# Retention and two feed-forward layers on one core: a negation moved, weights' stores one hop later, eight weight blocks kept on the chip

## The chip, the cores and the metric

The kernel runs on one core of one Trainium2 chip. The metric is the device time of one execution in microseconds (us). Five engines work side by side, each with its own instruction queue: TensorE (PE, matrix products), VectorE (DVE), ScalarE (ACT), GpSimd (POOL) and SyncE (SP), which in this kernel issues every transfer between the chip's memory (SBUF) and device memory (DRAM). Products accumulate in PSUM banks.

## The reference, cut to what matters

```
q, k, v: 4 batches, 8 heads, 576 positions, 64 per head
D[i, j]  = gamma_h ** (i - j) for i >= j, else 0
attn     = (q @ k.T / 8 * D) @ v                    # no softmax
x        = attn as 2304 tokens x 512
h        = x @ w_in                                 # 512 -> 2048
g        = max(h, 0) + alpha * min(h, 0)            # one alpha per unit
x2       = g @ w_out                                # 2048 -> 512
gate     = sigmoid(x2 @ w_gate); val = x2 @ w_val   # 512 -> 1536 each
out      = (gate * val) @ w_out2                    # 1536 -> 512
```

## The kernel before

**Numbers.** Each fp32 operand of a feed-forward product is split into a high and a low part, and a product is three matmuls (high by high, high by low, low by high; `products`, L632). `split` (L202, L203) makes the parts: ACT copies the source rounded (high), DVE subtracts that from the source (low).

**Tokens** are cut into blocks of 256, 512, 512, 512, 512. Block 0 and 1 run first, with the attention's chunks (up to 128 positions) in front of and between them; then block 2, in which the attention of 3 and 4 and the second layer's weights are prepared; then blocks 3 and 4 together in eight double steps (`h_step`), which use sums of weights and fewer products; then the y products of these, the second layer for the pairs of blocks, and block 0's second layer at the end.

**The attention.** `att_q` makes a decayed copy of q: ACT writes the factors `dec` (L497, two buffers), POOL multiplies q with it in place (L500). PE makes the scores s (L518), DVE masks them (L522), PE makes o and the state's update m (L537 to L557), DVE adds the update to m_sb (L551, L553), and `split` makes x from o.

**The first layer.** Its weights come as 16 column blocks of the first matrix (m = 0, 512 by 128, index f) and 16 row blocks of the second (m = 1). A block r is loaded as 64-bit words into one of five raw slots (`load_weight`, L217). `to_single` makes fp32 of it: two ACT passes (L225, L226), then on DVE a shift into a buffer (L229), an add (L231) and a sign insertion (L234). For m = 0 the buffer of the shift is also the result, `one`; for m = 1 the result is in the raw slot and the buffer, `top`, is free after the add. `one` and `top` share two buffers of the tag "top". `prepare_weight` then splits the result (ACT L248, DVE L250) into w and stores: `one` (256 KB) to w1f (L254), from which the double steps later make their sums, and the split block (512 KB) to w1d (L257), from which it is read again later. It is a generator; each `yield` ends a hop, and `advance` takes every open generator one hop further between pieces of PE's work. When one has ended, `load_weights` loads the next raw blocks into whatever raw slots are free.

`ffn1_h` makes one h tile (12 products of 4 column parts into a PSUM bank; two banks, ps_h), ACT the two halves of the leaky function (L651, L652), DVE joins them with the unit's −alpha from na_sb (L653), and `split` makes g. `ffn1_y` multiplies g with the row block into four accumulating banks.

**What stays.** 38 slots of 4 KB per partition (`slot`, `free`) serve everything in turn, freed ones going to the end of the line. `uses` counts how many blocks still read a weight: row and column blocks with f < 9 (RES) stay for three blocks, later ones are reloaded from w1d by `fetch`. The double steps take seven slots out (`quarter_slots`, NQ, twice); `load_inner(t)` reads into them, for q = 0 and 1, the split column block 2t+q and half of block 2t+q+8 from w1d, beside the sums that `prepare_sums` makes.

**Order.** PE's order is the program's. The other engines' orders are set by a scheduler when the program is built; `behind(...)` ties an instruction behind an urgent one of its engine (a split of x or g). SP issues its transfers in order: one that waits holds up those behind it.

**The negation.** The alphas are loaded last of the first inputs (L1139), and ACT makes na_sb = −alpha (L1140) right behind in the program.

Of the kernel before, what the change touches and what calls it, by code (L numbers as in the profile page):

```python
# [10 lines left out]
F32 = mybir.dt.float32  # L11
# [19 lines left out]
NSLOT = 38  # L31
NLATE, NWIDE = 2, 8
NRAW = 5
NQ = 7
AHEAD = 2


# [76 lines left out]
def retention_two_ffn(ctx: ExitStack, tc: tile.TileContext, att, cst, alpha, w1, w2, out0, out1):  # L114
# [57 lines left out]
    def free(t):  # L172
        h = held[t.tensor.name]
        h[1] -= 1
        if not h[1]:
            where, _, line = held.pop(t.tensor.name)
            line.append(where)
# [58 lines left out]
    def prepare_weight(key):  # L236
        layer, f, m = key
        raw = raw_w.pop(key)
        if m == 0:
            one = small.tile([P, DM], F32, tag="top", name=f"one{f}_{m}")  # L240
            yield from to_single(raw, one.bitcast(U32))
            free(raw)
        else:
            one = raw[:, :, 0].bitcast(F32)
            yield from to_single(raw)
        yield
        w = slot([P, 2, DM], F32R, f"w{layer}_{f}_{m}")
        nc.scalar.activation(w[:, 0, :], one, AF.Copy)  # L248
        yield
        nc.vector.tensor_tensor(out=w[:, 1, :], in0=one, in1=w[:, 0, :].bitcast(F32), op=ALU.subtract)  # L250
        wt[f, m] = w
        uses[f, m] = PLAIN if f < RES else 2 if f < BESIDE else 1
        if m == 0:
            nc.sync.dma_start(out=w1f[f % NSUM][:, f // NSUM], in_=one)  # L254
        else:
            free(raw)
        nc.sync.dma_start(out=w1d[f, m], in_=w.bitcast(F32))  # L257

    def used(f, m):

# [152 lines left out]
    def load_weights():  # L413
        while to_load and raw_slots:
            load_weight(to_load.pop(0))

    def advance():

        for g in list(under_way):
            with behind("act", "dve"):  # L420
                done = next(g, StopIteration) is StopIteration
            if done:
                under_way.remove(g)
                load_weights()

    def begin_weight():
        if to_prepare and to_prepare[0] in raw_w:
# [361 lines left out]
    def load_inner(t):  # L789

        for q in range(2):
            w = inner[t, q, 1] = slot([P, 2, DM], F32R, f"wi{t}_{q}", quarter_slots)
            nc.sync.dma_start(out=w.bitcast(F32), in_=w1d[2 * t + q, 0])
        w = inner[t, 0, 2] = inner[t, 1, 2] = slot([P, 2, 2, DM // 2], F32R, f"wi{t}_3", quarter_slots)
        for q in range(2):
            nc.sync.dma_start(out=w[:, q].bitcast(F32), in_=w1d[2 * t + q + NSUM, 0][:, :, DM // 2:])
# [3 lines left out]
    def h_step(t, between):  # L800
        bank = bank_of(f"h_{t}", t == 0)
        seen = {}

        def product(ps, m, q, first=False):
            i, place = INNER_AT[m]
            if i == 0:
                need(1, 2 * t + q)
            w = inner[t, q, i]
            if i == 0:
                w = tuple(x[:, place] for x in w)  # L810
            elif i == 1:
                w = tuple(w[:, x, place * 256:(place + 1) * 256] for x in range(2))
            else:
                w = tuple(w[:, q, x] for x in range(2))
            products(
                ps, [
                    (tuple(x[:, k * P:(k + 1) * P] for x in w), tuple(x[:, k] for x in factors[m]))
                    for k in range(2)
                ], first, True, True,
            )  # L820
            for key, n in ((q if i < 2 else 0, i), (4, 2, 2)[i]), (m, 2):
                seen[key] = seen.get(key, 0) + 1
                if seen[key] == n:
                    if key == m:
                        if t == NIN - 1:
                            for x in factors.pop(m):
                                free(x)
                        continue
                    w = inner.pop((t, *key))
                    for x in w if i == 0 else (w,):  # L830
                        free(x)

        for c in range(2):
            for r in range(2):
                gated[t, c, r] = slot([P, 2, DM], F32, f"g{t}_{c}{r}")
        a, b, c, e, es, d = {}, {}, {}, {}, {}, {}

        def out(ps, r, k):
            for q in range(2):
                leaky(gated[t, k, r][:, q], ps[q], 2 * t + q + k * NSUM, f"lt{t}_{r}{k}{q}")  # L840

        for m, q in ((1, 0), (5, 0), (5, 1), (1, 1)) if t == 0 else ((1, 0), (1, 1), (5, 0), (5, 1)):
            x = a if m == 1 else e
            x[q] = bank("ae"[m == 5], q)
            product(x[q], m, q, True)
            between(0)
        for q in range(2):
            b[q] = bank("b", q)
            nc.scalar.activation(b[q], a[q], AF.Copy)
            es[q] = small.tile([P, DM], F32, tag="es", name=f"hes{t}_{q}")  # L850
            nc.scalar.activation(es[q], e[q], AF.Copy)
        between(1)
        for q in range(2):
            product(a[q], 6, q)
            c[q] = bank("c", q)
            nc.vector.tensor_tensor(out=c[q], in0=a[q], in1=es[q], op=ALU.add)
        for q in range(2):
            product(b[q], 2, q)
        between(2)
        out(b, 0, 0)  # L860
        for q in range(2):
            product(a[q], 7, q)
        for q in range(2):
            d[q] = gated[t, 1, 1][:, q]
            nc.vector.tensor_tensor(out=d[q], in0=a[q], in1=es[q], op=ALU.add)
        for q in range(2):
            product(c[q], 3, q)
        between(3)
        out(c, 0, 1)
        for q in range(2):  # L870
            product(a[q], 4, q)
        between(4)

        out(a, 1, 0)
        with behind("act", "dve", ahead=0):
            out(d, 1, 1)
# [260 lines left out]
    for n in runs_of(0) + runs_of(1):  # L1137
        load_chunk(n)
    nc.sync.dma_start(out=al_sb, in_=alpha)  # L1139
    nc.scalar.activation(na_sb, al_sb, AF.Copy, scale=-1.0)  # L1140
    load_weights()

    pa, py = (ps_a, "ab"), (ps_y, "yy")
# [1 line left out]
    done = [0]  # L1145

    def first_h(i):
        while done[0] < EARLY and done[0] * (n0 + n1 - LATE) < EARLY * (i + 1 - LATE):
            ffn1_h(0, done[0])
            done[0] += 1  # L1150
# [43 lines left out]
    for j in range(1, PLAIN):  # L1194
        stages = stages_of(2) if j == 1 else stages_of(3, 4)
        first = step1 if j == 1 else 0
        total = 2 * sum(len(runs_of(i)) for i in ((2,) if j == 1 else (3, 4)))
        span = SPAN * (NF1 - first) // NF1 if j == 1 else SPAN_X
        staged = 0
        for f in range(first, NF1):  # L1200
            fetch(f, 0)
            fetch(f + 1, 0)
            fetch(f, 1)
            ffn1_h(j, f)
            if j < PLAIN - 1 or f < UNTIL:
                second_pace(PACE_S)
            if j == PLAIN - 1 and staged == total:
                if not under_left:

                    for _ in stages:  # L1210
                        pass
                    for x in "ab":
                        ps = ps_a.tile([P, DM], F32, tag=x, name=f"whole{x}")
                        nc.tensor.matmul(ps, wt[f, 1][:, 0, :P], x_t[j][:, 0, 0], start=True, stop=True)
                    att_only.close()
                    pool = ctx.enter_context(tc.tile_pool(name="late", bufs=1, reuse_waits="tile"))
                    spare.extend((pool, f"late{i}") for i in range(NLATE))
                    under_left.append(left_factors(-1))
                else:
                    next(under_left[0], None)  # L1220
            if j == PLAIN - 1 and f == UNTIL:
                quarter_slots.extend(spare.popleft() for _ in range(NQ))
                load_inner(0)
            if j == PLAIN - 1 and UNTIL <= f < UNTIL + 2:
                begin_job((1, f - UNTIL))
            for point in range(2):
                second_step()
                if staged < total and staged * span < total * (2 * (f - first) + point):
                    next(stages)
                    staged += 1  # L1230
                if point == 0:
                    later(BEHIND - 1)
                elif under_left:
                    next(under_left[0], None)
            late.append((j, f))
        for _ in stages:
            pass
# [2 lines left out]
    x_only.close()  # L1240
    pool = ctx.enter_context(tc.tile_pool(name="wide", bufs=1, side="right", reuse_waits="tile"))
    spare.extend((pool, f"wide{i}") for i in range(NWIDE))
    quarter_slots.extend(spare.pop() for _ in range(NQ))

    def in_h(t):
        def between(point):
# [159 lines left out]
```

## Time and profile before

| | before |
|---|---|
| three runs, median (lowest to highest) | 891.17 us (890.69 to 892.07) |
| the profiled execution | 890.89 us |
| its span, first to last instruction | 889.1 us |
| PE busy | 856.2 us, 96% |
| PE's weight loads, beside its products | 716.7 us, 81% |
| DVE, ACT, POOL busy | 566.2, 446.6, 126.5 us |
| moved by DMA | 245.05 MB |
| mean granted clock of PE | 0.995 |

Spans and waits of all views come from the profiled execution. An engine is busy in a row from its start for the length given; rows of one engine may overlap by a tenth of a us where the next starts while the last one drains. In brackets stands the idle time ahead of a row and what ended it. A wait for several things is put down to the one that came last.

### The profile page before, as it was taken

Reading aid. Unit: us, or ns where it says so; the run is one execution under the profiler, and the core shown is the slowest. Engines: PE = TensorE matmul, PEld = TensorE weight load, DVE = VectorE, ACT = ScalarE, POOL = GpSimd, SP = SyncE. Lnnn points to the kernel's source line nnn. Section 1 sums busy time; section 2 is a strip of 40 time slices with the busy share of each in tenths; the row PEclk is TensorE's granted clock in tenths of the full one; section 3 lists DMA queues with packets and bytes.
Section 4 is the critical chain, followed back from the end, with each engine's and each line's share of the span. In section 5 each row is a group of like instructions: output and inputs, shape, how many; then the busy total and the mean of one; then the engine's idle time right before and its main releaser. Section 6 shows DMA issues by size and latency. Waiting matters only on the chain.

```text
span 889.1 us, 13072 instructions
## 1 busy us (share of the span) xinstructions
PE 856.2 (96%) x4770; PEld 716.7 (81%) x4770; DVE 566.2 (64%) x829; ACT 446.6 (50%) x785; POOL 126.5 (14%) x119
## 2 busy tenths in 40 slices
PE   5689989999999999999999999999999999999998
PEld 4578878777887888887888878888888888888897
DVE  2798995577767578888945676368932333496121
ACT  4487874455644566787625555335432222353111
POOL 5100002334621001123531032000000000000000
PEclk9899999999999999999999999999999999999999
DMA  9779999779996545769995999916698563359970
GB/s 306 253 244 368 373 378 348 279 270 302 341 343 245 207 165 189 264 227 362 356 414 188 336 418 405 365 72 213 223 397 286 185 206 123 137 201 356 388 267 24
DMA packets 89679, 245.05 MB, mean 276 GB/s; under 512 B 13072, under 2 KB 16144, under 8 KB 89616
## 3 DMA queue, kind: packets, MB, share of 16 engines
q1 hardware_dynamic: 89616, 244.22, 75.6%
q8 instruction: 38, 0.62, 0.3%
q14 instruction: 25, 0.20, 0.1%
HBM read 176.03 MB, written 68.16 MB: 275 GB/s over the span
## 4 chain that ended last, share of the span: by engine, by line
PE 50%; DMA 5%; DVE 2%; ACT 2%; issue 1%; SPq 0%; ACTq 0%; DVEq 0%
PE a L637 13%; PE yy L637 10%; PE oa L637 7%; PE z L637 4%; PE e L637 3%; DMA r<-w 3%; PE b L637 3%; PE c L637 3%; PE o L637 2%; PE oc L637 2%; PE ob L637 2%; PE oe L637 2%; DMA tq<-td 1%; DMA wo<-wod 1%; DVE q L312 0%
## 5 line engine op out<-in xcount | busy, mean ns | idle before, releaser
L637 PE MATMUL h<-x,w 128*128 128x512 f32 (+1 forms) x432 | 85.5, 348 | 7.6 <-DVE g L203 5.8
L637 PEld LDWEIGHTS h<-x,w 128*128 128x128 f32 x432 | 67.6, 189 | 19.5 <-DVE g L203 7.3
L301 POOL TENSOR_TENSOR r<-r,r 128x256 f32<-128x256 f32 x36 | 46.1, 1288 | 242.7 <-DVE r L234 196.7
L312 DVE TENSOR_TENSOR q<-r,q 128x512 fp32r<-128x512 f32 x72 | 54.6, 784 | 16.2 <-ACT q L311 15.9
L311 ACT ACTIVATE q<-r 128x512 fp32r<-128x512 f32 x72 | 46.2, 671 | 28.7 <-POOL r L301 17.9
L637 PE MATMUL y<-g,w 128*128 128x512 f32 x240 | 58.9, 394 | 0.0
L653 DVE SCALAR_TENSOR_TENSOR h<-h,na_sb,t 128x512 f32<-128x512 f32 (+1 forms) x48 | 32.0, 667 | 37.0 <-ACT h L652 37.0
L225 ACT ACTIVATE r<-r 128x512 f32<-128x512 f32 x68 | 45.6, 670 | 15.7 <-DMA r<-w 15.6
L637 PEld LDWEIGHTS y<-g,w 128*128 128x128 f32 x240 | 44.4, 188 | 10.2 <-issue 1.0
L651 ACT ACTIVATE t<-h 128x512 f32<-128x512 f32 (+1 forms) x48 | 25.0, 521 | 53.9 <-PE h L637 53.8
L963 DVE TENSOR_TENSOR c<-a,es 128x512 f32<-128x512 f32 x24 | 16.7, 697 | 52.4 <-PE a L637 48.7
L226 ACT ACTIVATE r<-r 128x512 int32<-128x512 uint32 x68 | 45.5, 669 | 0.0
L500 POOL TENSOR_TENSOR qk<-qk,dec 128x512 f32<-128x512 f32 (+1 forms) x16 | 20.4, 1278 | 144.2 <-DMA qk<-att 139.0
L231 DVE CUSTOM_DVE_ANT_0 r<-r,top 128x1024 uint16<-128x1024 uint16 x52 | 37.4, 732 | 1.6
L234 DVE SCALAR_TENSOR_TENSOR r<-r 128x512 uint32<-128x512 uint32 x52 | 37.4, 724 | 0.5
L637 PEld LDWEIGHTS z<-x,zp 128*128 128x128 f32 x288 | 36.0, 192 | 0.9
L637 PE MATMUL z<-x,zp 128*128 128x256 f32 x288 | 36.3, 283 | 0.0
L637 PE MATMUL h<-x,v 128*128 128x512 f32 x144 | 35.4, 395 | 0.0
L637 PE MATMUL y<-g,v 128*128 128x512 f32 x144 | 35.2, 393 | 0.0
L202 ACT ACTIVATE g<-h 128x512 fp32r<-128x512 f32 (+1 forms) x48 | 25.1, 522 | 20.1 <-DVE h L653 19.9
L518 PE MATMUL s<-qk 64*128 64x128 f32 (+1 forms) x320 | 23.3, 285 | 12.3 <-POOL qk L500 7.3
L203 DVE TENSOR_TENSOR g<-h,g 128x512 fp32r<-128x512 f32 (+1 forms) x48 | 28.8, 599 | 9.5 <-ACT g L202 9.2
(460 smaller groups left out, 2246.6 us busy)
## 6 DMA issues: line engine op xcount, KB each, us to landing
tq<-td SPq DMA_DIRECT2D x84, 512.0 KB, 8.3
r<-w SPq DMA_DIRECT2D x68, 512.0 KB, 6.6
wo<-wod SPq DMA_DIRECT2D x42, 512.0 KB, 3.5
v<-w1d SPq DMA_DIRECT2D x40, 512.0 KB, 6.1
td<-q SPq DMA_DIRECT2D x36, 512.0 KB, 4.0
w1d<-w SPq DMA_DIRECT2D x32, 512.0 KB, 6.3
wod<-q SPq DMA_DIRECT2D x24, 512.0 KB, 9.6
zp<-td SPq DMA_DIRECT2D x48, 256.0 KB, 5.2
```

The source lines that it names most:

```text
L202: a = nc.scalar.activation(hi, src, AF.Copy)
L203: d = nc.vector.tensor_tensor(out=lo, in0=src, in1=hi.bitcast(F32), op=ALU.subtract)
L225: nc.scalar.activation(high.bitcast(F32), high.bitcast(F32), AF.Copy, scale=2.0 ** -112)
L226: nc.scalar.activation(low.bitcast(I32), low, AF.Copy, scale=2.0 ** -29)
L231: nc.vector.tensor_tensor(out=out.bitcast(I32), in0=low.bitcast(I32), in1=top.bitcast(I32), op=ALU.add)
L234: nc.vector.scalar_tensor_tensor(out, high, 0x80000000, out, ALU.bitwise_and, ALU.bitwise_or)
L301: sub = lambda o, a, b: nc.gpsimd.tensor_tensor(out=o, in0=a, in1=b, op=ALU.subtract)
L311: nc.scalar.activation(part[0], src, AF.Copy)
L312: nc.vector.tensor_tensor(out=part[1], in0=src, in1=part[0].bitcast(F32), op=ALU.subtract)
L637: nc.tensor.matmul(ps, l, r, start=first and i == 0, stop=last and i == len(todo) - 1, skip_group_check=joins)
L651: nc.scalar.activation(t, ps, AF.Relu)
L653: nc.vector.scalar_tensor_tensor(ps, ps, na_sb[:, f:f + 1], t, ALU.mult, ALU.add)
```

## The change

Three things are changed.

a) na_sb's negation is written into `first_h`, which runs between the attention's chunks, ahead of the first h tile, and tied behind ACT's last urgent split. On ACT it then stands behind the split of chunk 5's x and ahead of the first t.

b) In `prepare_weight`, `load_weights` is called where the raw slot becomes free (for m = 0 after the sign insertion, for m = 1 after the subtraction), no longer at the generator's end, and the two stores come one hop later.

c) The first eight column blocks (f < NSUM = 8) are not stored to w1d and are kept in their slots for one more use, in the double steps; `load_inner` no longer reloads them, and the slots taken out for the double steps are five (NQ1) in place of seven.

```diff
-NQ = 7
+NQ, NQ1 = 7, 5
@@ prepare_weight
             yield from to_single(raw, one.bitcast(U32))
             free(raw)
+            load_weights()
...
         wt[f, m] = w
-        uses[f, m] = PLAIN if f < RES else 2 if f < BESIDE else 1
+        stays = m == 0 and f < NSUM
+        uses[f, m] = PLAIN + stays if f < RES else 2 if f < BESIDE else 1
+        if m:
+            free(raw)
+            load_weights()
+        yield
         if m == 0:
             nc.sync.dma_start(out=w1f[f % NSUM][:, f // NSUM], in_=one)
-        else:
-            free(raw)
-        nc.sync.dma_start(out=w1d[f, m], in_=w.bitcast(F32))
+        if not stays:
+            nc.sync.dma_start(out=w1d[f, m], in_=w.bitcast(F32))
@@ advance
                 under_way.remove(g)
-                load_weights()
@@ load_inner
-            w = inner[t, q, 1] = slot([P, 2, DM], F32R, f"wi{t}_{q}", quarter_slots)
-            nc.sync.dma_start(out=w.bitcast(F32), in_=w1d[2 * t + q, 0])
+            inner[t, q, 1] = wt[2 * t + q, 0]
@@ h_step
+                    if i == 1:
+                        used(2 * t + q, 0)
+                        continue
@@ main program
-    nc.scalar.activation(na_sb, al_sb, AF.Copy, scale=-1.0)
     load_weights()
@@ first_h
+        if i == LATE:
+            with behind("act", ahead=0):
+                nc.scalar.activation(na_sb, al_sb, AF.Copy, scale=-1.0)
@@ two places, ahead of the double steps
-                quarter_slots.extend(spare.popleft() for _ in range(NQ))
+                quarter_slots.extend(spare.popleft() for _ in range(NQ1))
...
-    quarter_slots.extend(spare.pop() for _ in range(NQ))
+    quarter_slots.extend(spare.pop() for _ in range(NQ1))
```

PE's order is the same before and after. The order of the other engines moves. In the listings below, lines are those of each version (L250 and L653 of before are L251 and L659 of the change), the two numbers behind a weight's name are its f or m as far as the name keeps them (r_6_0 is column block 6, r_5_1 row block 5), and the last number is the buffer's; one_0_894 of before and one_0_888 of the change are the `one` of block 6.

ACT, at the end of the attention's first chunks, before:

```order
L497 ACTIVATE dec_1784<-c_sb 128x128 x4
L1140 ACTIVATE na_sb<-al_sb 128x16
L497 ACTIVATE dec_1899<-c_sb 128x128 x4
L202 ACTIVATE x_243<-o_327 128x4x128
L225 ACTIVATE r_0_0_230<-r_0_0_230 128x512
```

and with the change, there and at the first h tile:

```order
L503 ACTIVATE dec_1776<-c_sb 128x128 x4
L503 ACTIVATE dec_1891<-c_sb 128x128 x4
L202 ACTIVATE x_242<-o_326 128x4x128
L225 ACTIVATE r_0_0_229<-r_0_0_229 128x512
...
L202 ACTIVATE x_305<-o_517 128x4x128
L1158 ACTIVATE na_sb<-al_sb 128x16
L657 ACTIVATE t_0_553<-h_0_540 128x256
```

The first two dec rows shown are those of chunks 7 and 8, x of o_327 or o_326 is chunk 1's, x of o_517 chunk 5's. The negation left the place between dec of chunk 7 and dec of chunk 8 and stands ahead of the first tile's t.

DVE from the sign insertion of block 6's `one` to that of block 7's, before (the names in brackets are what a row waits for; DMAHW is a transfer):

```order
L234 SCALAR_TENSOR_TENSOR one_0_894<-r_6_0_758,one_0_894 128x512 [waits DVE_49]
L229 TENSOR_SCALAR top<-r_5_1_798 128x512 [waits DMAHW5_49,DMAHW1_49]
L203 TENSOR_TENSOR g_3_852<-h_3_835,g_3_852 128x512 [waits Activation_49]
L231 ISA r_5_1_798<-r_5_1_798,top 128x512x2 [waits DVE_49]
L250 TENSOR_TENSOR w_6_0_924<-one_0_894,w_6_0_924 128x512 [waits Activation_49]
L234 SCALAR_TENSOR_TENSOR r_5_1_798<-r_5_1_798 128x512 [waits DVE_49]
L229 TENSOR_SCALAR one_0_951<-r_7_0_830 128x512 [waits DMAHW4_49]
L653 SCALAR_TENSOR_TENSOR h_4_897<-h_4_897,na_sb,t_4_910 128x256 [waits Activation_49]
```

and with the change:

```order
L234 SCALAR_TENSOR_TENSOR one_0_888<-r_6_0_753,one_0_888 128x512 [waits DVE_49]
L659 SCALAR_TENSOR_TENSOR h_3_831<-h_3_831,na_sb,t_3_844 128x512 [waits Activation_49]
L251 TENSOR_TENSOR w_4_1_886<-r_4_1_695,w_4_1_886 128x512 [waits Activation_49]
L229 TENSOR_SCALAR top<-r_5_1_758 128x512 [waits DMAHW4_49,DMAHW1_49]
L251 TENSOR_TENSOR w_6_0_920<-one_0_888,w_6_0_920 128x512 [waits Activation_49]
L203 TENSOR_TENSOR g_3_848<-h_3_831,g_3_848 128x512 [waits Activation_49]
L231 ISA r_5_1_758<-r_5_1_758,top 128x512x2 [waits DVE_49]
L659 SCALAR_TENSOR_TENSOR h_4_891<-h_4_891,na_sb,t_4_904 128x256 [waits Activation_49]
L229 TENSOR_SCALAR one_0_944<-r_7_0_824 128x512 [waits DMAHW6_49,DMAHW3_49,DVE_49]
```

Block 7's shift into `one_0_944` now waits for two transfers, its own load and the store of block 6's `one`; before, it waited for one.

SP in the same stretch, before:

```order
L217 DMA r_8_0_919<-w 128x1024
L254 DMA w1f_130<-one_0_894 128x512
L217 DMA r_7_1_943<-w 128x1024
L257 DMA w1d_0_104<-w_6_0_924 128x1024
L257 DMA w1d_1_103<-w_5_1_949 128x1024
```

and with the change:

```order
L217 DMA r_7_1_917<-w 128x1024
L262 DMA w1f_130<-one_0_888 128x512
L217 DMA r_8_0_912<-w 128x1024
L264 DMA w1d_1_101<-w_4_1_886 128x1024
L217 DMA r_8_1_972<-w 128x1024
```

The store of block 6's `one` stands behind the load that takes the slot of its raw block, and the column block's split store is gone.

## Rows read from the trace of the kernel before

**Rows 1.** one core, busy us (instructions) by engine, PEclk, DMA share, GB/s, by windows

```profile
40.00:60.00 20.00, 16.20 (x131) 13.79 (x130) 17.98 (x37) 14.77 (x31) 0.00 (x0) 1.00 0.79 282
80.00:100.00 20.00, 19.27 (x115) 17.14 (x116) 18.45 (x36) 15.45 (x31) 0.00 (x0) 1.00 1.01 383
140.00:160.00 20.00, 20.00 (x124) 17.77 (x124) 6.13 (x11) 8.94 (x23) 4.60 (x4) 1.00 0.94 341
...
160.00:280.00 120.00, 116.75 (x940) 93.71 (x942) 86.51 (x139) 62.59 (x128) 47.96 (x46) 1.00 0.85 302
```

**Rows 2.** PE's waits: engine, line, releaser, total us, times, longest

```profile
PE h L637 <- DVE g L203: 5.8, 5, 1.8
```

**Rows 3.** PE's timeline: start, us, what, idle before it

```profile
27.43 0.86 PE L518 MATMUL s<-qk 64*64 64x64 f32 x13 [3.79 <-DVE x L203]
...
59.26 3.01 PE L637 MATMUL h<-x,w 128*128 128x512 f32 x12 [1.83 <-DVE g L203]
...
92.21 3.02 PE L637 MATMUL h<-x,w 128*128 128x512 f32 x12 [0.44 <-DVE g L203]
...
125.90 3.03 PE L637 MATMUL h<-x,w 128*128 128x512 f32 x12 [1.61 <-DVE g L203]
...
401.42 0.50 PE L637 MATMUL a_h<-xx_4h,s7h 128*128 128x512 f32 x1 [0.52 <-DVE g L865]
```

**Rows 4.** DVE's timeline, 60 to 90 us: two waits

```profile
68.54 0.43 DVE L229 TENSOR_SCALAR top<-r 128x512 uint32<-128x512 uint32 x1 [0.93 <-issue]
...
82.49 0.43 DVE L229 TENSOR_SCALAR top<-r 128x512 uint32<-128x512 uint32 x1 [1.25 <-DMA w1f<-one]
```

**Rows 5.** ACT's timeline, 17 to 50 us

```profile
18.98 1.28 ACT L497 ACTIVATE dec<-c_sb 128x128 f32<-128x128 f32 x4 [1.23 <-POOL qk L500]
24.79 0.21 ACT L1140 ACTIVATE na_sb<-al_sb 128x16 f32<-128x16 f32 x1 [4.53 <-DMA al_sb<-alpha]
24.91 1.26 ACT L497 ACTIVATE dec<-c_sb 128x128 f32<-128x128 f32 x4
```

**Rows 6.** POOL's timeline, 17 to 32 us

```profile
18.21 0.73 POOL L500 TENSOR_TENSOR qk<-qk,dec 128x256 f32<-128x256 f32 x1 [0.24 <-DMA qk<-att]
...
23.50 0.72 POOL L500 TENSOR_TENSOR qk<-qk,dec 128x256 f32<-128x256 f32 x1
```

**Rows 7.** DVE's timeline, 72 to 81 us: how long its rows take

```profile
73.29 0.75 DVE L653 SCALAR_TENSOR_TENSOR h<-h,na_sb,t 128x512 f32<-128x512 f32 x1
73.95 0.68 DVE L250 TENSOR_TENSOR w<-r,w 128x512 fp32r<-128x512 f32 x1
74.55 0.69 DVE L234 SCALAR_TENSOR_TENSOR one<-r,one 128x512 uint32<-128x512 uint32 x1
...
77.89 0.42 DVE L229 TENSOR_SCALAR one<-r 128x512 uint32<-128x512 uint32 x1
78.23 0.49 DVE L653 SCALAR_TENSOR_TENSOR h<-h,na_sb,t 128x256 f32<-128x256 f32 x1
78.62 0.68 DVE L231 CUSTOM_DVE_ANT_0 one<-r,one 128x1024 uint16<-128x1024 uint16 x1
...
79.82 0.42 DVE L203 TENSOR_TENSOR g<-h,g 128x256 fp32r<-128x256 f32 x1
```

**Rows 8.** transfers, us to landing: w1f stores issued at 30.38, 53.30, 63.04, 75.55

```profile
w1f<-one SPq DMA_DIRECT2D x1, 256.0 KB, 2.4
...
w1f<-one SPq DMA_DIRECT2D x1, 256.0 KB, 4.1
...
w1f<-one SPq DMA_DIRECT2D x1, 256.0 KB, 5.4
...
w1f<-one SPq DMA_DIRECT2D x1, 256.0 KB, 6.9
```

**Rows 9.** the chain of waits ahead of 401 us

```profile
370.73 4.60 DMA r<-w
```

**Rows 10.** SP's timeline at 267 us

```profile
267.72 0.51 SPq L368 DMA_DIRECT2D b<-w1f  x1
```

## Prediction

> **What bounds the kernel now.** I read the 20 us windows of the first 160 us, then PE's waits, then the timelines of the engines that end them, last the chain of waits. TensorE (PE) is busy 20.00 of 20 us in 140 to 160 and idle for 3.25 us (120.00 − 116.75) in all of 160 to 280 [rows 1], after that only at 401, which is treated below. The change leaves PE's order as it is, so it can only move idle time, and most of that lies ahead of 140. There, between 60 and 140, DVE is the busiest of the others: 18.45 us in 80 to 100, with the DMA engines at a share of 1.01 [rows 1]. PE waits there for DVE's split of g, 5.8 us in five waits [rows 2]: 1.83 us at 59.26, 0.44 at 92.21, 1.61 at 125.90 [rows 3], the other two lie between. PE works an h tile ahead of its y products, and ps_h has two banks, so h tile k needs the g of tile k−2 out of its bank. Whatever delays DVE ahead of those g's lands on PE; DVE's own waits there are 0.93 us at 68.54 and 1.25 us at 82.49 [rows 4], both the shift that opens a weight's preparation and needs a buffer of "top". What an earlier step buys before 125.90 is kept only as far as the next g permits.
>
> **Part a, the negation.** ACT stands 4.53 us before na_sb, waiting for alpha's transfer; dec of chunk 8 and the split of chunk 1's x are queued behind it [rows 5], and PE's next scores wait 3.79 us for that split's DVE half [rows 3]. It looks like 4.5 us to be had. It isn't: dec has two buffers, and dec of chunk 8 takes that of chunk 6, which POOL reads from 23.50 for 0.72, to 24.22 [rows 6]. The pair before shows the step: dec of chunk 7 started at 18.98, right after POOL had ended with the buffer [rows 5]. So dec starts at about 24.26 in place of 24.91, and x's split comes **0.65 us** earlier, not 4.5. In its new place, ahead of the first t, the negation costs ACT 0.12 us (24.79 to 24.91); alpha has long landed by then, so it adds no wait.
>
> **Part b in the attention.** In the rows of 20 to 60 two things differ besides: x of chunk 6 has 1.20 us less of DVE rows ahead of it, and the first matrix's loads are issued a hop sooner. Followed by hand with the old durations, the first h tile of block 1 starts 1.95 us earlier and the split of g(1,1), for which 59.26 waits, 0.65 to 1.2 us earlier; I take **−0.9 us** for PE at 59.26.
>
> **Part b, the stores one hop later.** No store is taken away by this, but the shift's buffer is. A column block's single-precision copy `one` lies in "top"; its store w1f reads it, and the next user but one of the buffer must wait until that store has landed. DVE's rows, from start to start [rows 7]: 0.66 for L653 at 512 columns and 0.39 at 256, 0.60 for the other rows of 512 (73.95 to 74.55), 0.34 for a shift and, being as long (0.42), for g's split at 256. Before, one6's store had 6.00 us of such rows to land in, and still cost 1.25; one4's had 4.60 and cost 0.93. Afterwards the shift of one7 waits for one6's store, with seven rows between (0.66 + 0.60 + 0.34 + 0.60 + 0.60 + 0.60 + 0.39 = **3.79 us**), and that of r_7_1 for one7's, with eight (0.60 + 0.60 + 0.39 + 0.60 + 0.60 + 0.34 + 0.34 + 0.60 = **4.07 us**); one4's keeps 4.60, all others have 5.5 or more. Each store also stands behind one load on SP that the same DVE row releases, about 0.55 us.
>
> So all hangs on how long a 256 KB store takes to land, L. It took 2.4 us when issued at 30.38, 4.1 at 53.30, 5.4 at 63.04, 6.9 at 75.55 [rows 8]. The bytes decide: per pair of weights the kernel of before moves 512 × 4 + 256 KB, and without the column block's split store 512 × 3 + 256, 22% less, until block 8; a DMA share of 1.01 in 80 to 100 would become some 0.8. With a like share, 0.79 in 40 to 60 [rows 1], stands the store of 53.30. I take L = **4.1 us**, and 2.4 and 6.9 as bounds.
>
> The Trainium skill, page "DMA: Bandwidth & Descriptors", section "Anatomy of one DMA — SWDGE (gpsimd) path", gives about 2.0 us fixed plus bytes over 436 GB/s, which for 256 KB is an estimate of 2.6 us. The store of 30.38 agrees with 2.4, that of 75.55, with 6.9, doesn't; by the page's figure none of the new waits would arise, and the time would be that of rival B.
>
> With L = 4.1: one7's shift waits 0.55 + 4.1 − 3.79 = 0.86, r_7_1's 0.55 + 4.1 − 4.07 = 0.58, together 1.44; the old 0.93 + 1.25 = 2.18 go. DVE's order has more weights' rows ahead of some g's: +2.14 us ahead of g(0,6) (for which 92.21 waits), +0.94 ahead of g(0,11) (for which 125.90 waits). At 92.21: −0.9 − 2.18 + 1.44 + 2.14 = +0.5 us, PE later. At 125.90: −0.9 − 2.18 + 1.44 + 0.94 = **−0.7 us** if DVE then has its h in time; PE's +0.5 of 92.21 has waits of 0.73 and 1.61 left in which to disappear, yet DVE takes h from PE, so some of it stays: 0 to −0.7, I take **−0.35**. Each us more of L costs two waits in series at 125.90, and from 4.05 on one4's as a third.
>
> **Part c, eight blocks kept.** Eight stores and eight loads of 512 KB go, 8.4 of 245 MB. In the double steps PE is fed but for one wait of 0.52 at 401.42, for DVE's g [rows 3]; the chain of waits leads to it over a load of r (370.73, 4.60 us) [rows 9] and a store of td. None of these is removed; eight loads fewer lie beside them. Bounds: 0, and 0.7 (the 0.52 and a little around it); I take **−0.3**, since DVE's order there is unchanged and its own rows come between those transfers. The price: slots. Eight are held to the double steps, two of them in place of quarter slots. The load of b on SP at 267.72 [rows 10] comes some 2 us later, because it stands behind a v load that now waits for a slot; its users on DVE come later too, and PE's next need of them is ten us on. I cost this at nothing, and 0.5 to 1 if the cover is gone. The 3.25 us of 160 to 280 I leave as they are: DVE's rows stand in the old order there but for a few.
>
> **Sum.** The profiled execution took 890.89 (span 889.1 and 1.8 around it), 0.28 under the median of 891.17. 890.89 − 0.35 − 0.3 = **890.2 us**.
>
> **Rivals.** *B, the stores land fast.* With L = 3.6 the two waits are 0.36 and 0.08: −0.9 − 2.18 + 0.44 + 0.94 = −1.7 at 125.90, and −0.3 to −0.7 at 401: 888.5 to 888.9. For it: 22% fewer bytes, 2.4 us on an empty queue. Against: r's load of 512 KB goes out just ahead of each store.
>
> *C, the other side: the stores stay slow.* The place is DVE's shifts of one7 and r_7_1, the price 2 to 3 us per us of L; at L of about 4.4 the gain of 125.90 is gone, and from about 5.2 the slowing can be measured. With the 5.4 of 63.04 [rows 8] the waits are 2.16, 1.88 and, at one4's, 1.35, 5.39 in place of 2.18, so −0.9 + 3.21 + 0.94 = +3.2: 890.89 + 3.2 − 0.3 = 893.8. For it: stores of 5.4 to 6.9 in just that stretch of before.
>
> *D, the slots.* b's loads and the td stores behind them come late enough for PE to wait: +0.5 to 1 on the forecast, 890.7 to 891.2.
>
> *E, the negation was the bottleneck after all.* If dec of chunk 8 needn't wait for POOL, x's split comes up to 4.5 us sooner, PE's 3.79 goes, and what the weights' loads let through of it, 1 to 3 us, is kept: 887 to 889. Against it stands the two-buffer rule and the row of 18.98.
>
> **Chances.** Forecast 0.38, D 0.12, B 0.22, E 0.06, C 0.22. What a measurement of this kernel can tell from no change is about 0.2%, 1.78 us: faster is under 889.4, slower over 892.95. B and E, and 0.05 of the forecast, lie below: faster 0.33. Of C 0.19 lies above, the rest is between: slower 0.19, same 0.48. The range leaves out C's upper half and E: **888.2 to 893.6**.
>
> **What would show it.** Right: dec of chunk 8 starting at about 24.3; na_sb without a wait; PE at h(1,2) at 58.3 to 58.7; DVE's shifts of one7 and r_7_1 waiting for a w1f store, by 0.5 to 1 us each, and w1f's landing at 4 us; PE's gap at 401 within 0.5 us of what it was. Wrong: stores of 5 us and more between 60 and 100 (C), none of these waits (B), PE gaps between 160 and 300 that end with a DMA (D).

## The result and the profile after

The changed kernel is slower: 899.12 us (median of 6 runs, 897.60 to 900.95) against 891.66 for the kernel before (6 runs), a ratio of 1.0083 with a 95% interval of 1.0066 to 1.0100. Forecast were 890.2 and a range of 888.2 to 893.6. The profiled execution took 900.35 with a span of 898.6; before these were 890.89 and 889.1.

PE's order is the same in both kernels, so the start of one and the same product can be subtracted between the traces. The first fence is PE's timeline of the changed kernel at the places of [rows 3] (start, us, what, idle time ahead and what ended it) and at four more.

```profile
26.16 0.68 PE L524 MATMUL s<-qk 64*64 64x64 f32 x14 [3.31 <-DVE x L203]
...
57.94 3.06 PE L643 MATMUL h<-x,w 128*128 128x512 f32 x12 [1.83 <-DVE g L203]
80.21 4.28 PE L643 MATMUL h<-x,w 128*128 128x512 f32 x12 [2.08 <-DVE g L203]
94.83 3.01 PE L643 MATMUL h<-x,w 128*128 128x512 f32 x12 [1.51 <-DVE g L203]
104.94 3.06 PE L643 MATMUL h<-x,w 128*128 128x512 f32 x12 [1.51 <-DVE g L203]
...
129.60 3.03 PE L643 MATMUL h<-x,w 128*128 128x512 f32 x12 [0.93 <-DVE g L203]
...
203.49 0.51 PE L643 MATMUL h<-x,w 128*128 128x512 f32 x1 [1.22 <-ACT x L202]
...
286.01 1.64 PE L543 MATMUL o<-qk,m_sb 128*128 128x128 f32 x8 [2.05 <-DVE qk L528]
...
411.10 0.50 PE L643 MATMUL a_h<-xx_4h,s7h 128*128 128x512 f32 x1 [0.57 <-DVE g L873]
```

| the product that started before at | starts after at | difference |
|---|---|---|
| 59.26 | 57.94 | −1.32 |
| 80.30 | 80.21 | −0.09 |
| 92.21 | 94.83 | +2.62 |
| 125.90 | 129.60 | +3.70 |
| 198.22 | 203.49 | +5.27 |
| 278.02 | 286.01 | +7.99 |
| 401.42 | 411.10 | +9.68 |
| the end (span) | | +9.5 |

So PE is 1.3 us early at 58, 5.0 are lost between 58 and 130, and another 6.0 between 130 and 411. The profiled execution is 1.2 us above the median of its kernel and that of before 0.8 under its own, so 2.0 of the 9.5 belong to these two executions. The 1.3 isn't a gain of the change: the product that starts at 8.9 us in the trace of before starts 1.11 earlier here, and 0.6 to 1.4 earlier in each of the other twelve traces, whatever was changed in them.

The first loss is seen in the windows (busy us of PE, PEld, DVE, ACT, POOL, then granted clock, DMA share, GB/s). To set against [rows 1]:

```profile
80.00:100.00 20.00, 18.28 (x95) 15.75 (x96) 16.83 (x34) 15.78 (x32) 0.00 (x0) 0.91 0.79 266
100.00:120.00 20.00, 17.78 (x111) 15.81 (x110) 17.79 (x33) 14.99 (x32) 0.00 (x0) 1.00 0.99 369
```

The DMA share of 80 to 100 fell from 1.01 to 0.79, as reckoned; yet PE did 95 products there in place of 115, and DVE lost time too: 16.83 busy in place of 18.45. DVE's timeline tells on what it stood (the answer to [rows 4]), and the three stores behind that, in the order of their issue at 62.09, 74.02 and 81.49 (the answer to [rows 8]; last column us to landing):

```profile
68.84 0.43 DVE L229 TENSOR_SCALAR top<-r 128x512 uint32<-128x512 uint32 x1 [2.55 <-ACT w L249]
...
78.19 0.43 DVE L229 TENSOR_SCALAR one<-r 128x512 uint32<-128x512 uint32 x1 [0.81 <-DVE h L659]
...
86.88 0.43 DVE L229 TENSOR_SCALAR top<-r 128x512 uint32<-128x512 uint32 x1 [1.72 <-DMA w1f<-one]
```

```profile
w1f<-one SPq DMA_DIRECT2D x1, 256.0 KB, 6.7
...
w1f<-one SPq DMA_DIRECT2D x1, 256.0 KB, 4.1
...
w1f<-one SPq DMA_DIRECT2D x1, 256.0 KB, 5.3
```

The first two waits are put down to another engine, but each ends within 0.1 us of a store's landing: 62.09 + 6.7 = 68.8 and 74.02 + 4.1 = 78.1. These are the three shifts of the prediction, of r_4_1, one7 and r_7_1: 5.08 us in all, where 2.18 had been.

After the wait of 2.08 at 80.21 the granted clock fell to half, to 1.2 GHz (column behind POOL's):

```profile
82.00:83.00 1.00, 1.00 (x3) 0.72 (x3) 1.00 (x3) 0.64 (x2) 0.00 (x0) 0.50 0.87 164
...
288.00:290.00 2.00, 2.00 (x30) 1.97 (x26) 1.20 (x3) 0.10 (x1) 0.00 (x0) 0.53 0.00 0
```

The twelve products at 80.21 took 4.28 us in place of 3.01, and with their successors PE lost 1.6 us there beside its waits. The second row is the stretch behind the wait of 2.05 at 286.01, where another 1.6 went the same way (from +7.99 at 278.02 to +9.58 at the product that started before at 290).

What ACT shows of the moved negation (the answer to [rows 5]):

```profile
23.62 1.28 ACT L503 ACTIVATE dec<-c_sb 128x128 f32<-128x128 f32 x4 [4.03 <-POOL qk L506]
24.80 0.57 ACT L202 ACTIVATE x<-o 128x512 fp32r<-128x512 f32 x1
...
40.49 0.20 ACT L1158 ACTIVATE na_sb<-al_sb 128x16 f32<-128x16 f32 x1
```

ACT stands nearly as long as before (4.03 in place of 4.53), and now for POOL; the negation runs at 40.49 without a wait.

### The profile page after: what moved, and what is told of

It is laid out like the page before. It is cut to its first block, busy times and chain, and to the rows that moved or that the text cites. A ratio compares the mean times of both kernels' runs of the same rounds, so it can differ in the third digit from the quotient of the medians.

```text
span 898.6 us, 13045 instructions
## 1 busy us (share of the span) xinstructions
PE 859.9 (96%) x4770; PEld 719.7 (80%) x4770; DVE 569.1 (63%) x829; ACT 446.9 (50%) x785; POOL 127.3 (14%) x119
## 4 chain that ended last, share of the span: by engine, by line
PE 53%; DMA 3%; DVE 2%; ACT 1%; issue 1%; SPq 0%; ACTq 0%; DVEq 0%
PE a L643 14%; PE yy L643 10%; PE oa L643 7%; PE z L643 4%; PE b L643 4%; PE e L643 4%; PE c L643 3%; PE o L643 2%; PE oc L643 2%; PE ob L643 2%; PE oe L643 2%; DMA r<-w 2%; DMA wo<-wod 1%; DMA td<-q 0%; DVE g L772 0%
## 5 line engine op out<-in xcount | busy, mean ns | idle before, releaser
L659 DVE SCALAR_TENSOR_TENSOR h<-h,na_sb,t 128x512 f32<-128x512 f32 (+1 forms) x48 | 32.0, 667 | 35.4 <-ACT h L658 35.3
L643 PEld LDWEIGHTS y<-g,w 128*128 128x128 f32 x240 | 44.8, 189 | 10.5 <-issue 1.0
L234 DVE SCALAR_TENSOR_TENSOR r<-r 128x512 uint32<-128x512 uint32 x52 | 40.3, 779 | 0.4
L308 POOL TENSOR_TENSOR r<-r 128x256 f32<-128x256 f32 x36 | 34.6, 966 | 3.0 <-DVE r L234 1.4
```

Source lines behind the costliest of these rows:

```text
L234: nc.vector.scalar_tensor_tensor(out, high, 0x80000000, out, ALU.bitwise_and, ALU.bitwise_or)
L308: sub = lambda o, a, b: nc.gpsimd.tensor_tensor(out=o, in0=a, in1=b, op=ALU.subtract)
L643: nc.tensor.matmul(ps, l, r, start=first and i == 0, stop=last and i == len(todo) - 1, skip_group_check=joins)
L659: nc.vector.scalar_tensor_tensor(ps, ps, na_sb[:, f:f + 1], t, ALU.mult, ALU.add)
```

## The experiments

Theory 1 was rival C's: stores one hop later that land late hold the shift's buffer. Theory 2 was rival D's: the slots of the kept blocks. Each part of the change was first put alone into the kernel before, and the waits were taken out of the changed kernel. Ratios are to the kernel before, run beside each (medians of 891.7 to 893.4), with their 95% intervals. "Lost at 125.9" is how much later the product of 125.90 starts than in the profile of before; each is taken from one execution.

**e1, the negation alone.** The diff is that of part a.

> The kernel before with the negation alone moved. Theory 1 (the loss comes from the stores one hop later: a store of 'one' that lands late holds the shift buffer): dec of chunk 8 starts 0.5 to 0.7 us earlier, and 891.7 moves by less than 1 us either way. Theory 2 (the loss comes from the slots that the eight kept blocks hold): the same. Rival E of the prediction (the negation was the bottleneck): 1 to 3 us faster.

890.67 us, ratio 0.9984 (0.9968 to 0.9999), so the part is harmless. By the time alone rival E isn't out, since 890.67 is 1.6 under the 892.23 of before beside it. The trace speaks against it: dec of chunk 8 takes over the wait (ACT's timeline, 17 to 45 us), and PE's wait for x behind it is 3.09 us in place of 3.79.

```profile
23.15 1.28 ACT L497 ACTIVATE dec<-c_sb 128x128 f32<-128x128 f32 x4 [4.33 <-POOL qk L500]
```

**e2, the stores one hop later alone.** The diff is that of part b, with the stores of all 32 split blocks.

> The kernel before with the loads a hop sooner and the stores a hop later alone; all 32 split stores stay. Theory 1: slower by 3 to 6 us, DVE's shifts waiting 4 us and more in all between 60 and 125 us for a w1f store, as the changed kernel does. Theory 2: within 1 us of before, and no more shift waits than the 2.2 us of before.

891.48 us, ratio 0.9983 (0.9967 to 0.9999); the product of 125.90 is 1.8 us early. DVE's waits (engine, line, releaser, total, times, longest; 40 to 140 us):

```profile
DVE h L655 <- ACT h L654: 4.6, 9, 1.1
DVE top L229 <- DMA w1f<-one: 2.2, 2, 1.6
```

The shifts wait 2.2 us for stores, as they did before (0.93 and 1.25), and not the 5 of the changed kernel. DVE now waits most for h, which means that it is no longer the late one. Theory 1 as it stood falls: the later stores by themselves neither bring those waits nor lose anything. What 5 us of them would cost, this run can't tell.

**e3, the kept blocks alone.** The diff is that of part c; loads and stores stay at their old hops.

> The kernel before with the eight blocks kept, alone; loads and stores at their old hops. Theory 1: no new waits ahead of 140 us, since each w1f store goes out as before with fewer bytes beside it; 890 to 892.5, what it loses is between 240 and 290 us, up to 2 us. Theory 2: most of the changed kernel's loss, 5 to 8 us slower, with PE's waits between 150 and 300 us.

899.86 us, ratio 1.0086 (1.0057 to 1.0115): the whole loss. But it isn't where theory 2 has it. PE's waits between 46 and 140 us:

```profile
PE h L639 <- DVE g L203: 10.5, 8, 2.0
```

10.5 us in place of 5.8, and the product of 125.90 is 4.5 us late. At that time no kept block holds a slot longer than before, since every one of them still has its three plain uses ahead. Both theories missed this run.

**e4, buffers of its own for `one`, in the changed kernel.**

```diff
-            one = small.tile([P, DM], F32, tag="top", name=f"one{f}_{m}")
+            one = small.tile([P, DM], F32, tag="es", name=f"one{f}_{m}")
```

> The changed kernel, but 'one' lies in two buffers of its own (those of a tag that is not used before the double steps), so that no shift of a row block waits for a store. Theory 1: the shift waits of 5 us go, PE is at the h tile of 129.6 us some 3 to 5 us earlier, and the time falls from 899.1 to 893 to 896. Theory 2: 898 to 900, as the changed kernel.

897.05 us, ratio 1.0053 (1.0033 to 1.0073); lost at 125.9: 2.3. No shift waits for a store here, and the kernel gets back 2 to 3 of its 7.5 us (2.1 by the medians, 0.3% by the ratios), not 3 to 5. That isn't the price of the waits alone: the same edit moves DVE's order, as the table below shows (+4.28 ahead of g(0,11) in place of +0.94).

**Theory 1b** came from a count over DVE's order. I added up, from the lists of DVE's instructions in the order in which they are built into each kernel and with the durations of [rows 7], the work that stands ahead of each g's split, against the kernel before. The column "shift waits" was read off the traces: DVE's idle time ahead of its shifts (L229) between 55 and 126 us that ends within 0.15 us of the landing of a w1f store; in the kernel before it is 2.18.

| rows ahead of, us more than before | g(0,6) | g(1,5) | g(0,10) | g(0,11) | shift waits | lost at 125.9 |
|---|---|---|---|---|---|---|
| the changed kernel | +2.14 | +2.74 | +0.94 | +0.94 | 5.37 | 3.7 |
| e2, stores later alone | −0.94 | −1.20 | −2.40 | −3.08 | 2.23 | −1.8 |
| e3, kept blocks alone | +2.74 | +2.74 | +5.82 | +4.28 | 3.43 | 4.5 |
| e4, own buffers | +3.34 | +2.74 | +5.82 | +4.28 | 0 | 2.3 |
| e5, slots alone | 0 | 0 | 0 | 0 | 3.98 | 0.7 |
| e6, no split stores | +2.74 | +2.74 | +5.82 | +4.28 | 4.05 | 3.7 |
| e7, weights tied closer | 0 | +0.60 | 0 | 0 | 4.19 | 2.0 |
| e8, without kept blocks | −0.94 | −1.20 | −2.40 | −3.08 | 2.40 | −3.6 |

DVE works in order and PE waits for its g's. With eight stores fewer, the scheduler that sets the order when the kernel is built brings weights' preparation forward on DVE, ahead of g's that PE needs sooner; the later hop pushes it back, and the changed kernel has some of both.

How far does the count carry? Ahead of 126 us DVE's order is the same, row by row, in groups of these traces. With the order of before (before itself, e1, e5, e10) PE is 2.0 early to 0.7 late at 125.9; with that of e2 (e2, e8, e9, e12) 1.5 to 3.6 early; with that of e3 (e3, e6) 3.7 and 4.5 late. So the order goes with gain or loss, and traces of one and the same order differ by 0.9 to 2.7 us. The rows alone don't give the size: the changed kernel with +0.94 and e7 with 0 lose more than they should, e4 with +4.28 less. Added to the shift waits beyond 2.18 they come closer: +4.1 for the changed kernel, +2.0 for e7, +2.1 for e4, −2.9 for e8. In e2 (−3.0, measured −1.8), e3 (+5.5, measured 4.5), e5 (+1.8, measured 0.7) and e6 (+6.2, measured 3.7) they miss by 1 us and more. This sum was made after the runs, and none of them tests it.

Part c divides into two halves: held slots with the old order, and the new order without held slots.

**e5, slots alone.** Part c without the lines that leave out the eight stores.

> The kernel before with the eight blocks held to the double steps and not reloaded, but all 32 split stores left in; DVE's order is then word for word that of before up to the h tile of 125.9 us. Theory 1b (without the eight stores the scheduler puts weights' rows on DVE ahead of the g's for which PE waits, 2.7 us of rows at 92.2 and 4.3 at 125.9): no loss ahead of 140, at most 0.7 us; what is lost is lost between 240 and 300 us, 1 to 3 us, so 892.5 to 895. Theory 2 (slots): most of the 7.6 us of kept blocks alone, 897 to 900.

893.01 us, ratio 1.0018 (1.0001 to 1.0035). As theory 1b has it: the loss ahead of 126 is small, and b, held up on SP behind a wait for a slot, costs a wait of DVE of 1.5 us and one of PE of 1.29 (timelines, 278 to 284 us):

```profile
279.10 0.69 DVE L338 TENSOR_TENSOR s<-b 128x512 f32<-128x512 f32 x1 [1.53 <-DMA b<-w1f]
...
283.01 1.13 PE L538 MATMUL o<-qk,m_sb 128*128 128x128 f32 x8 [1.29 <-DVE qk L523]
```

In the changed kernel the same DVE row waits 2.27, and b is issued at 274.75 in place of 267.72 [rows 10].

Most of what this profile lost stands elsewhere: PE is 0.7 late at 125.9 and 3.3 at the product of 139.9, since behind a wait of 3.08 the granted clock fell to half (PE's timeline, then the window). This execution took 895.64, 2.6 above the median of its ten, so that loss is not taken for the edit's.

```profile
126.64 5.49 PE L638 MATMUL h<-x,w 128*128 128x512 f32 x12 [3.08 <-DVE g L203]
...
126.00:133.00 7.00, 6.36 (x15) 5.02 (x16) 6.40 (x13) 5.10 (x11) 0.00 (x0) 0.51 1.02 410
```

**e6, no split stores.** The other half:

```diff
-            nc.sync.dma_start(out=w.bitcast(F32), in_=w1d[2 * t + q, 0])
+            nc.sync.dma_start(out=w.bitcast(F32), in_=w1d[2 * t + q + NSUM, 0])
...
-        nc.sync.dma_start(out=w1d[f, m], in_=w.bitcast(F32))
+        if not (m == 0 and f < NSUM):
+            nc.sync.dma_start(out=w1d[f, m], in_=w.bitcast(F32))
```

> The other half: the eight split stores are left out and no block is kept; the double steps load the split blocks 8 to 15 in place of 0 to 7, so that part of the output is computed with other weights and the work is the same. DVE's order up to 125.9 us is that of the kept blocks alone. Theory 1b: PE is 4 to 5.5 us later at the h tile of 125.9 than before, nothing is lost between 240 and 300, in all 4 to 6 us slower: 896 to 898. Theory 2: 891 to 893, fewer bytes and no loss.

897.03 us, ratio 1.0077 (1.0050 to 1.0103); lost at 125.9: 3.7. Less traffic, no held slot, and nearly the whole loss, where theory 2 expected 891 to 893: most of the loss belongs to the eight missing stores and not to the slots. PE still waits 0.85 at 283.63, so not all of that late wait belongs to the slots; 3.7 is below the 4 to 5.5 expected.

**e7, weights tied closer, in the changed kernel.**

```diff
-AHEAD = 2
+AHEAD = 1
```

> The changed kernel with AHEAD at 1 in place of 2: weights' rows are tied behind the urgent split one place later, which leaves 0 to 0.6 us more rows ahead of the g's of 92.2 and 125.9 us than before, in place of 2.1 and 0.9, and 2 to 3 us fewer up to 80 us. Theory 1b: PE gets back 2 to 4 us by 130 us, 895 to 897.5. If only the late stores count: no gain, 898 to 900.

893.31 us, ratio 1.0016 (1.0000 to 1.0032): it takes back 5.8 of 7.5, more than the 2 to 4 expected. Its profile doesn't bear out the whole path, though. PE is 4.8 us early at 59.26, 2.0 late at 125.9 (3.7 in the changed kernel), and only 0.8 late at 278.02 (8.0 there). Of the 7.2 us that PE has over the changed kernel at 278.02 only 1.7 are there at 125.9. The constant ties the second layer's preparation too, so the greater part of this gain belongs to orders that I did not count. The stores stay out in this run and only orders move, which is the best sign that the stores act through an order.

**e8, without the kept blocks.** Parts a and b together.

> The changed kernel without the kept blocks: negation and stores a hop later, 32 stores, reloads. DVE has 0.9 to 3.1 us fewer rows of weights ahead of the g's from 92.2 to 125.9 us than before. Both theories: no slower than before; 1b: PE at the h tile of 125.9 is 1.5 to 2.5 us earlier than before, and 889.5 to 891.5 in all.

890.84 us, ratio 0.9980 (0.9965 to 0.9996). PE is 3.6 us early at 125.9 and 4.5 at 193.8, and then gives 2.7 back in one place (ACT's and PE's timelines, 194 to 197 us). Behind it the granted clock is 0.50 from 197 to 200, and by 278 all but 0.15 is gone.

```profile
194.82 1.07 ACT L499 ACTIVATE dec<-c_sb 128x64 f32<-128x64 f32 x4 [4.30 <-POOL qk L502]
195.79 0.57 ACT L202 ACTIVATE x<-o 128x512 fp32r<-128x512 f32 x1
```

```profile
196.42 0.51 PE L639 MATMUL h<-x,w 128*128 128x512 f32 x1 [2.65 <-ACT x L202]
```

It is the pattern of part a once more: a dec that waits for POOL's use of its buffer, with a split behind it for which PE waits.

**e9, e10, e11: every dec behind the last split.** In e9 (on e8), e10 (on the kernel before) and e11 (e9 with AHEAD at 1):

```diff
-                nc.scalar.activation(by[:, pr, :c], ...)
+                with ExitStack() if n < len(runs_of(0) + runs_of(1)) + 1 else behind("act", ahead=0):
+                    nc.scalar.activation(by[:, pr, :c], ...)
```

The number that n is compared with is 8; `...` stands for the rest of the call, which is the same.

> The negation and the stores a hop later, no kept blocks, and dec of chunks 8 and up tied behind the last split of x on ACT. Without the tie (the run before of that kernel) ACT stood 4.3 us before dec of a chunk at 194.8 us, with the split behind it for which PE waited 2.6 us, and PE lost there 2.7 of the 3.6 us it had gained by 125.9. If the split's place behind dec is the cause: no wait of over 1 us for ACT's x at the first h tile of block 2, 887 to 889.5. If dec then comes too late for its scores, waits of PE for POOL's qk take its place: 890.5 to 893. For the first chunks: x of chunk 1 no longer stands behind dec of chunk 8, so its split comes with its product, and PE's wait there falls from 3.3 us to under 2.

> The kernel before with that tie alone. There the negation still stands ahead of x of chunk 1, and the wait at the first h tile of block 2 was 0.3 us, so little is to be had: 890.5 to 893, within 0.2 per cent of before. If the tie makes dec late: waits of PE for POOL's qk of 1 us and more, slower by 1 to 3 us.

> As the first run of these, with AHEAD at 1 in place of 2. DVE has 1 to 3 us fewer rows of weights ahead of the g's up to 80 us, and 0 to 3 fewer after. If those rows set PE's time up to 130 us: PE another 0.5 to 1.5 us earlier at the h tile of 125.9, and 886 to 889. If weights then come late for PE's products: no gain or a loss of 1 to 2 us.

908.84, 907.11 and 893.08 us, ratios 1.0178 (1.0159 to 1.0196), 1.0165 (1.0146 to 1.0185) and 1.0012 (0.9998 to 1.0026): three misses. e9 and e10 lose far more than was allowed for the bad case, and e11 gains nothing. PE's waits of e9 from 140 to 330, and from 15 to 140:

```profile
PE s L521 <- POOL qk L503: 16.2, 6, 6.8
```

```profile
PE o L540 <- DVE m_sb L554: 6.2, 1, 6.2
```

The tie makes each dec so late that POOL's q and PE's scores wait for it; in e11 such waits come to 5.2 us from 15 to 330, and why they are so much shorter with AHEAD at 1 isn't explained. The second row speaks against rival E once more: with dec of chunk 8 out of the way, PE's wait for x of chunk 1 goes, and the next one, for the update of m_sb, grows from 2.85 to 6.2 us.

**e12, one dec behind one split.** On e8, the tie for chunk 14 alone, and seven urgent rows back:

```diff
+                with behind("act", ahead=7) if n == 14 else ExitStack():
```

> The negation and the stores a hop later, no kept blocks, and on ACT a single exchange: dec of chunk 14 (not needed until 40 us later) stands behind the split of chunk 10's x instead of ahead of it; no other row of ACT and none of DVE moves. In the run without the exchange ACT waited 4.3 us ahead of that dec, at 194.8 us, and PE 2.6 us for the split behind it. If that queueing is what gave back the gain of the stores' order: PE's wait for ACT's x at the first h tile of block 2 falls from 2.6 to under 0.5 us, and the time from 890.8 to 887 to 889.5, 0.3 to 0.5 per cent under before. If the split is late for another reason (its product, or ACT's other rows): 890 to 892, as without it.

888.90 us, ratio 0.9951 (0.9932 to 0.9970). The split no longer stands behind the dec, and PE's wait is gone (ACT's timeline, 193 to 197 us):

```profile
193.96 0.60 ACT L202 ACTIVATE x<-o 128x512 fp32r<-128x512 f32 x1 [1.27 <-PE o L560]
195.93 1.07 ACT L500 ACTIVATE dec<-c_sb 128x64 f32<-128x64 f32 x4 [1.38 <-POOL qk L503]
```

This beats both kernels, with parts a and b, without part c. The gain rests on the times: the profiled execution, the slowest of the six, has PE only 0.75 us ahead of before at 278.02, where e8 has 0.15.

## Why the prediction was wrong, point by point

**The bound** was read rightly: PE waits for DVE's g's ahead of 140. So was the sentence that an early gain is kept only as far as the next g permits: e11 has PE 8.4 us early at 59.26 and 1.9 at 125.90, e7 4.8 early and then 2.0 late.

**Part a** held. dec started at 23.62, right behind POOL, and x's split came no sooner than that; e1 shows no loss. The −0.9 at 59.26 measured −1.32, but that is luck: 1.11 of it stands there at 8.9 us already, and e5, with neither part a nor part b, has −1.23.

**Part c failed, and with it the sum.** It was costed at −0.3, by its transfers, with slots at nothing; alone it costs 0.86% or 7.7 us (e3). The step that failed is that leaving the eight stores out was priced as traffic only, and not by what it does to DVE: without held slots it still costs 0.77% (e6), with the stores left in 0.18% (e5). The extra rows on DVE (+2.14, +0.94) were read off the changed kernel, booked under part b, and taken at two g's only. Had the parts' orders been listed apart, part b alone would have shown −3.08 and part c alone +4.28 ahead of g(0,11). In between, ahead of g(1,5), the changed kernel has +2.74, which the sum left out; the h tile that takes that g's bank waits 1.51 at 104.94, where the kernel before had no wait. e3 and e6 show that DVE's order moves when the stores are missing, and e5 that it doesn't when they are there. That this order is what loses is argued, from the count and from e7: no run leaves the stores out and keeps DVE's order.

**The landing time L was the second step that failed.** Taken was 4.1 for all; the three stores took 6.7, 4.1 and 5.3, and DVE's shifts waited 5.08 us in place of 1.44. The rule by which the waits were worked out held: with the landing times measured (6.67, 4.09, 5.26) it gives 2.62, 0.85 and 1.74, and the waits were 2.55, 0.81 and 1.72. one7's wait came as forecast; the one that was put at nothing, behind one4's store, is the longest. The bytes fell as reckoned, but each of these stores stands right behind a load of 512 KB and lands 0.6 to 0.7 us after it (that of 62.09 at 68.8, the load issued at 61.71 at 68.1). With the measured waits the prediction's own sum gives −0.9 − 2.18 + 5.08 + 0.94 = +2.9 at 125.90, and the clock adds 1.6, which it had in no term; measured was +3.70 in place of −0.35. Rival C had this price, 5.39, and its +3.2. What C lacked is where it comes from: the later stores alone bring no such waits (2.2 us in e2, 2.4 in e8), and e3, without them, has the whole loss. How much of the changed kernel's loss is theirs, and how much the rows', no run separates, since e4 moves both.

**Slots and clock.** Rival D was right in kind: e5 loses 0.2% (0.01 to 0.35), and its trace has the wait for b. In the changed kernel it came on top of everything else at 286.01, 2.05 us and then 1.6 at half the clock, where 0.5 to 1 had been allowed. A fall of the clock behind a wait was in no term. At 401.42 the hoped-for −0.3 did not come: the wait is 0.57 in place of 0.52.

**Its chances** gave 0.19 to slower. Two losses that were each seen, the late stores and the slots, were weighed as rivals that exclude one another; in the changed kernel both are seen.

**What stays open.** Why the scheduler brings the weights forward without the eight stores I have only argued: a split store waits on SP for DVE's subtraction, and the next load stands behind it. No run isolates that. The gain of e7 past 130 us isn't explained, and the 1.2 us by which PE's wait for x at 203.49 grew in the changed kernel was not tested on that kernel itself. The same wait stands in e3 (1.24) and e6 (1.00) and not in e5, so it goes with the missing stores.

## What to carry to other kernels

Where a scheduler orders an in-order engine, a change that only takes transfers away can still move work on it: list that order for each part of the change, and add up what stands ahead of every row for which the bound engine waits, not of two of them, together with what that engine will stand idle for. Give each store the landing time of its own place: in all these traces a w1f store issued right behind a load landed after that load, by 0.4 us or more, though it moves half the bytes. Before a difference between two traces is put down to an edit, look at what runs with the same order differ by. A long wait on one engine is worth nothing until it is known what the next instruction in its queue would wait for.

## What the hardware showed that was not expected

Leaving the split blocks' stores out lowered the DMA share of 80 to 100 us from 1.01 to 0.79, and of the small stores between 60 and 90 those of blocks 6 and 7 took less time to land (4.1 and 5.3 us in place of 6.9 and 6.8), those of 4 and 8 more (6.7 and 4.1 in place of 5.4 and 3.6). PE's clock fell to 0.50 behind a wait of 2.08 us in the changed kernel at 80.21, but not behind the wait of 1.83 at 57.94; the products that followed cost 1.6 us, nearly as much as the wait itself. The length of the wait doesn't tell the two apart: in e2 the twelve products behind a wait of 1.82 at 57.98 took 4.61 us at the same low clock. And with the same order on DVE and PE it fell in one execution and not in another: e1 has 0.50 from 80 to 83 us, e5 0.51 from 126 to 133, and the profile of before 1.00 in both.
